# Softmax of the first q group moved partly onto ScalarE, searched ranks and later loads in an attention + feed-forward kernel

## Chip, cores and metric

One core of a Trainium2 chip. The metric is the device time of one execution in microseconds (us); a smaller time is better.

## What is computed

Linear attention with two softmaxes, then a feed-forward layer with a sigmoid-approximated gelu. q, k, v are float32 of shape 8 x 8 x 576 x 64 (batch, heads, rows, columns); the two weight matrices are float64.

```python
q_s = softmax of q over the last axis (64 columns), denominator + 1e-09
k_s = softmax of k over axis 2 (576 rows), denominator + 1e-09
kv  = einsum('bhsd,bhse->bhde', k_s, v)
x   = einsum('bhsd,bhde->bhse', q_s, kv), as 4608 rows x 512 columns
h   = x @ w_in                                # 512 x 2048
out = (h * (1 / (1 + exp(-1.702 * h)))) @ w_out   # 2048 x 512
```

## The kernel before

The 4608 rows are worked off in 12 blocks `t` of 384 rows (128 partitions x 3). Blocks 0 and 1 are special: their k, q and v are loaded in two groups of 4 heads each (`ek`, `eq`, `ev`, in memory that later holds weights), the later blocks in groups of 2 heads.

For a batch, `k_max` takes the maximum of k over rows (three VectorE steps and one reduction over partitions on GpSimd), `k_sub` subtracts it (L418, L421) and exponentiates on ScalarE (L424, L425), and `kv_pairs` multiplies k and v on TensorE (L465), with a column of ones for the sums, whose reciprocals (L470, L471) scale the result as ScalarE copies it out (L481). For a block, `q_soft` does the softmax of q for one group: maximum (L502) and subtraction (L503) on VectorE, one exponential over the whole group on ScalarE (L506), then sum, add, reciprocal and product on VectorE (L509 to L512). `q_tr` transposes (L529, copied out at L536), `x_pairs` multiplies by kv (L575 in the first two blocks), and `x_out` splits the result into a rounded part on ScalarE (L544) and a remainder on VectorE (L547).

The feed-forward layer takes 16 steps `j` per block: `g1` (L604, 12 matmuls of 384 columns; gelu at L610, rounding at L613, remainder at L616), and `g2` (L636, three pieces `c` of three matmuls of 512 columns). Both use split operands, so each product is three matmuls. Each of the 32 weight tiles (`wi0` to `wi15`, `wo0` to `wo15`, 512 KB each) arrives as float64 words and is converted once by `conv_w`: ScalarE L251, VectorE L255, L259 and L260, ScalarE L264, VectorE L270.

What sets the order: every step is entered in a list (`Plan.add`) with engine, cost, the buffers that it reads and writes, and a rank. `Plan.order` runs a small model of the engines (constants `HOP, LAND, RATE, ISSUE, TABLE`, L24) in which an engine that is free takes the ready step of lowest rank. The order in which steps begin in that model is the order in which the instructions are written, and each engine then works its own list strictly in that order. All loads are issued by SyncE (SP). Blocks 0 and 1 share steps 0 to 31 or so: `step_rank` lets their `g1` and `g2` alternate.

Of the kernel before, what the change touches and what calls it, by code (L numbers as in the profile page):

```python
# [18 lines left out]
class Plan:  # L19
# [1 line left out]

    HOP, LAND, RATE, ISSUE, TABLE = 0.1, 1.8, 270e3, 0.5, 1.28  # L24

    def __init__(self):
        self.ops = []
# [19 lines left out]
    def order(self):  # L47
        ops = self.ops
        left = [len(o[2]) for o in ops]
        users = [[] for _ in ops]  # L50
        for n, o in enumerate(ops):
            for d in o[2]:
                users[d].append(n)
        engines = sorted({o[0] for o in ops})
        free = dict.fromkeys(engines, 0.0)
        ready = {e: [] for e in engines}
        coming = []
        at = [0.0] * len(ops)
        for n, o in enumerate(ops):
            if not left[n]:  # L60
                heapq.heappush(ready[o[0]], (o[3], n))
        wire, table = 0.0, None
        began = []
        self.start = {}
        now = 0.0
        while len(began) < len(ops):
            while coming and coming[0][0] <= now:
                _, n = heapq.heappop(coming)
                heapq.heappush(ready[ops[n][0]], (ops[n][3], n))
            moved = False  # L70
            for e in engines:
                if free[e] > now or not ready[e]:
                    continue
                _, n = heapq.heappop(ready[e])
                _, cost, _, _, _, needs, size = ops[n]
                if needs is not None and needs != table:
                    cost, table = cost + self.TABLE, needs
                free[e] = done = now + cost
                if size:
                    wire = max(wire, done) + size / self.RATE  # L80
                    done = wire + self.LAND
                began.append(n)
                self.start[n] = now
                moved = True
                for u in users[n]:
                    left[u] -= 1
                    hop = 0.0 if ops[u][0] == e and not size else self.HOP
                    at[u] = max(at[u], done + hop)
                    if not left[u]:
                        heapq.heappush(coming, (at[u], u))  # L90
            if not moved:
                times = [f for e, f in free.items() if f > now and ready[e]]
                if coming:
                    times.append(coming[0][0])
                now = min(t for t in times if t > now) if any(t > now for t in times) else now
        return began


def dve(n, psum=False):
    return 0.15 + n / 960  # L100

# [6 lines left out]
def efficient_attention_then_gelu_ffn(  # L108
# [27 lines left out]
    ST = S - SM  # L136
    W = D + 1
    JOIN = 9

    const = ctx.enter_context(tc.tile_pool(name="const", bufs=1))  # L140
    psum = ctx.enter_context(tc.tile_pool(name="psum", bufs=1, space=bass.MemoryType.PSUM))
# [4 lines left out]
    def sb(name, shape, dtype=F32, tag=None):  # L146
        return const.tile(shape, dtype, name=name, tag=tag or name)
# [135 lines left out]
    def bc(a, n):  # L283
        return a.unsqueeze(len(a.shape)).broadcast_to([*a.shape, n])
# [4 lines left out]

    kbuf, vbuf, qbuf, tbuf = {}, {}, {}, {}  # L290

    def load_tail(b, rank):
        if b in etail:
            (kl, vl), tag = etail[b]
            keys = ((tag, 0), (tag, "v"))
        else:
            (kl, vl), keys = tail[0], ((("tail"), 0), (("tail"), 1))
        tbuf[b] = kl, vl, keys

        def run_k():  # L300
            nc.sync.dma_start(out=kl[0:ST], in_=k[b, :, SM:S, :].rearrange("h p d -> p h d"))  # L301

        def run_v():
            nc.sync.dma_start(out=vl[0:ST, :, 0:D], in_=v[b, :, SM:S, :].rearrange("h p d -> p h d"))  # L304

        plan.add("SP", plan.ISSUE, (), (keys[0],), rank, run_k, size=ST * H * D * 4)
        plan.add("SP", plan.ISSUE, (), (keys[1],), rank + 0.01, run_v, size=2 * ST * H * D * 4)

    def load_k(b, i, rank):
        n = group(b)  # L310
        t, key = ek[b, i] if b < 2 else (kt_[i], ("kt", i))
        kbuf[b, i] = t, key
        hs = slice(n * i, n * (i + 1))

        def run():
            nc.sync.dma_start(
                out=t.rearrange("p h c d -> p h (c d)"),
                in_=k[b, hs, 0:SM, :].rearrange("h (p c) d -> p h (c d)", c=CM),
            )

        plan.add("SP", plan.ISSUE, (), (key,), rank, run, size=n * SM * D * 4)

    def load_v(b, i, rank):
        n = group(b)
        t, key = ev[b, i] if b < 2 else (vt_[i], ("vt", i))
        vbuf[b, i] = t, key

        def run():
            if b < 2:
                nc.sync.dma_start(  # L330
                    out=t.rearrange("p h c d -> p h (c d)"),
                    in_=v[b, n * i : n * (i + 1), 0:SM, :].rearrange("h (p c) d -> p h (c d)", c=CM),
                )
                return
            for h in range(n):
                nc.sync.dma_start(
                    out=t[:, h, :, 0:D], in_=v[b, n * i + h, 0:SM, :].rearrange("(p c) d -> p c d", c=CM)
                )

        if b < 2:  # L340
            plan.add("SP", plan.ISSUE, (), (key,), rank, run, size=n * SM * D * 4)
        else:
            plan.add("SP", n * 0.6, (), (key,), rank, run, size=1.5 * n * SM * D * 4)

    def parts(t):

        t0 = t * TB
        b, s0 = divmod(t0, S)
        n = min(TB, S - s0)
        got = [(b, s0, 0, n // C)]  # L350
        if n < TB:
            got.append((b + 1, 0, n // C, P))
        return got
# [6 lines left out]
    def load_q(t, i, rank):  # L360
        n = group(t)
        qt, key = eq[t, i] if t < 2 else (qt_[i % 2], ("qt", i % 2))
        qbuf[t, i] = qt, key
        runs = [(0, 1, 1), (1, 0, 1)] if turned(parts(t)[0][0], i) else [(0, 0, n)]

        def run():
            for b, s0, p0, p1 in parts(t):
                for o, h, m in runs:
                    src = q[b, n * i + h : n * i + h + m, s0 : s0 + (p1 - p0) * C, :]
                    if t < 2:  # L370
                        nc.sync.dma_start(
                            out=qt[p0:p1].rearrange("p h c d -> p h (c d)"),
                            in_=src.rearrange("h (p c) d -> p h (c d)", c=C),
                        )
                    else:
                        nc.sync.dma_start(
                            out=qt[p0:p1, :, o : o + m], in_=src.rearrange("h (p c) d -> p c h d", c=C)
                        )

        plan.add("SP", plan.ISSUE * len(parts(t)) * len(runs), (), (key,), rank, run, size=n * TB * D * 4)  # L380

    nm = [0]
    maxes = {}
# [100 lines left out]

    nr = [0]
    rs = [sb(f"r{i}", [P, NP]) for i in range(2)]
    qm = [sb(f"qm{i}", [P, 4 * C]) for i in range(2)]

    def q_soft(t, i, ranks):
        n = group(t)  # L490
        qt, key = qbuf[t, i]
        M = ("qm", i % 2)
        dst, nkey = qt, key
        if t < 2:
            m = qm[i % 2].rearrange("p (h c) -> p h c", h=n)
            qn, nkey = qbuf[t, i] = en[t, i]
            dst = qn.rearrange("p c h d -> p h c d")
        else:
            m = qm[i % 2][:, : n * C].rearrange("p (c h) -> p c h", c=C)

        def run_m():
            nc.vector.tensor_reduce(out=m, in_=qt, axis=AX.X, op=ALU.max)  # L502
            nc.vector.tensor_tensor(out=qt, in0=qt, in1=bc(m, D), op=ALU.subtract)  # L503

        def run_e():
            nc.scalar.activation(qt, qt, AF.Exp)  # L506

        def run_s():
            nc.vector.tensor_reduce(out=m, in_=qt, axis=AX.X, op=ALU.add)  # L509
            nc.vector.tensor_scalar_add(m, m, 1e-9)  # L510
            nc.vector.reciprocal(m, m)
            nc.vector.tensor_tensor(out=dst, in0=qt, in1=bc(m, D), op=ALU.mult)  # L512

        e = n * C * D
        plan.add("DVE", 2 * dve(e), (key,), (key, M), ranks[0], run_m)
        plan.add("ACT", act(e), (key,), (key,), ranks[1], run_e, table="exp")
        plan.add("DVE", 2 * dve(e) + 0.35, (key,), (nkey, M), ranks[2], run_s)
# [234 lines left out]
    for rank, _, f, a in sorted(tasks, key=lambda s: s[:2]):  # L752
        if f in (load_k, load_v, load_q, k_max, k_sub, q_tr, x_pairs, g1, g2, load_w, conv_w, load_tail):
            f(*a, rank)
        else:
            f(rank)

    with tc.manual_schedule():
        for n in plan.order():
            plan.ops[n][4]()  # L760
# [24 lines left out]
```

## Time and profile before

| | |
|---|---|
| device time, median of 3 runs (range) | 916.12 us (915.61 to 918.11) |
| the profiled execution's own time | 916.58 us |
| its span, first to last instruction | 914.7 us |
| mean granted TensorE clock | 0.994 of full speed |
| TensorE busy | 885.1 us |
| VectorE, ScalarE busy | 390.2 us, 487.8 us |

The profiled execution is 0.46 us above the median; what lies around its span is 1.9 us. The profile page gives busy time per engine, a picture of the span in 40 slices, the chain of work that ended last, and the groups of instructions by source line. Times within the trace count from the start of the span.

### The profile page before, as it was taken

The page shows a single profiled execution, that of the slowest core. Times are in us where ns is not written, and L with a number is a line of the kernel's source. Part 1 is how long each engine was busy: PE and PEld are TensorE (multiplying, and loading weights), DVE is VectorE, ACT ScalarE, POOL GpSimd, SP SyncE. Part 2 cuts the span into 40 slices and gives each one's busy share as a digit, 9 for nine tenths or more (in the row PEclk, how much of TensorE's full clock was granted, in tenths as well). Part 3 has the DMA queues.
Part 4 walks back from the last instruction along what each step waited for, and adds up shares of the span by engine and source line. Part 5 has one row for each costly group of instructions (what it writes and reads, how often), then busy time and mean ns, then how long its engine had stood idle before and what let it go on. Part 6 is the DMA issues. An engine that isn't in the chain of part 4 may idle for free.

```text
span 914.7 us, 13010 instructions
## 1 busy us (share of the span) xinstructions
PE 885.1 (97%) x5200; PEld 785.7 (86%) x5200; DVE 390.2 (43%) x826; ACT 487.8 (53%) x840; POOL 27.8 (3%) x35
## 2 busy tenths in 40 slices
PE   2879999999999999999999999999999999999998
PEld 2668989888988988989889889888988898998897
DVE  8899996162531641341541352332263134132111
ACT  3776669464952763552773583544494265253222
POOL 1100001000100100000000010000010000000000
PEclk9899999999999999999999999999999999999999
DMA  9996000111310400000400320000141000000000
GB/s 257 353 315 208 1 1 1 52 53 31 100 40 14 120 11 35 18 18 35 122 18 34 85 55 35 18 18 35 33 100 42 9 18 9 36 18 1 35 1 35
DMA packets 94620, 55.37 MB, mean 61 GB/s; under 512 B 67424, under 2 KB 87904, under 8 KB 94560
## 3 DMA queue, kind: packets, MB, share of 16 engines
q1 hardware_dynamic: 94560, 54.54, 21.0%
q8 instruction: 41, 0.67, 0.3%
q14 instruction: 19, 0.16, 0.1%
HBM read 45.09 MB, written 9.44 MB: 60 GB/s over the span
## 4 chain that ended last, share of the span: by engine, by line
PE 93%; DMA 4%; SPq 2%; DVE 1%; ACT 0%; issue 0%; DVEq 0%
PE bank L636 44%; PE bank L604 44%; PE bank L465 2%; PE bank L529 1%; PE bank L580 1%; DMA raw<-in_moe_w_out 1%; DMA raw<-in_moe_w_in 1%; DMA ek<-in_k 1%; SPq L226 0%; PE bank L575 0%; SPq L221 0%; DVE tmp L260 0%; SPq L304 0%; DVE tmp L259 0%; SPq L330 0%; SPq L301 0%
## 5 line engine op out<-in xcount | busy, mean ns | idle before, releaser
L604 PE MATMUL bank<-xh,w 128*128 128x384 f32 x1536 | 429.0, 341 | 4.6 <-ACT w L264 3.5
L636 PE MATMUL bank<-w,gh 128*128 128x512 f32 x1152 | 366.6, 399 | 0.0
L604 PEld LDWEIGHTS bank<-xh,w 128*128 128x128 f32 x1536 | 282.0, 189 | 14.7 <-ACT w L264 3.9
L616 DVE TENSOR_TENSOR gl<-g,gh 128x384 fp32r<-128x384 f32 x192 | 106.6, 556 | 385.0 <-ACT gh L613 384.3
L610 ACT ACTIVATE g<-bank 128x384 f32<-128x384 f32 x192 | 94.5, 492 | 326.8 <-PE bank L604 326.0
L604 PE MATMUL bank<-xl,w 128*128 128x384 f32 x768 | 259.7, 338 | 0.0
L636 PEld LDWEIGHTS bank<-w,gh 128*128 128x128 f32 x1152 | 214.5, 189 | 41.1 <-issue 4.4
L636 PE MATMUL bank<-w,gl 128*128 128x512 f32 x576 | 228.4, 397 | 0.0
L604 PEld LDWEIGHTS bank<-xl,w 128*128 128x128 f32 x768 | 144.9, 189 | 7.0
L636 PEld LDWEIGHTS bank<-w,gl 128*128 128x128 f32 x576 | 108.7, 189 | 25.8
L613 ACT CAST gh<-g 128x384 fp32r<-128x384 f32 x192 | 98.5, 513 | 6.3 <-PE bank L636 0.3
L610 ACT ACT_TABLE_LOAD x54 | 69.3, 1283 | 1.0
L502 DVE TENSOR_REDUCE qm<-qt 128x6 f32<-128x384 f32 x40 | 22.0, 551 | 67.2 <-DMA qt<-in_q 67.2
L506 ACT ACT_TABLE_LOAD x36 | 46.2, 1283 | 1.9 <-DMA qt<-in_q 1.3
L403 POOL PARTITION_ALL_REDUCE mx<-mx x24 | 21.0, 876 | 611.1 <-DVE mx L399 611.1
L536 ACT COPY qT<-bank 128x384 f32<-128x384 f32 x48 | 22.7, 476 | 29.8 <-PE bank L529 29.6
L509 DVE TENSOR_REDUCE qm<-qt 128x6 f32<-128x384 f32 x40 | 22.0, 550 | 25.7 <-ACT qt L506 25.6
L424 ACT ACT_TABLE_LOAD x18 | 23.1, 1283 | 5.5 <-DMA ek<-in_k 5.2
L465 PE MATMUL bank<-ev,ek 128*64 128x64 f32 x128 | 7.2, 273 | 19.0 <-ACT eq L506 12.4
L547 DVE TENSOR_TENSOR xl<-bank,xh 128x384 fp32r<-128x384 f32 x48 | 24.0, 550 | 3.0 <-ACT xh L544 3.0
L481 ACT ACTIVATE kvn<-bank,r 64x64 f32<-64x64 f32 x64 | 17.9, 306 | 14.0 <-DVE r L471 12.2
L251 ACT ACTIVATE tmp<-raw 128x512 f32<-128x512 f32 x32 | 21.2, 673 | 5.7 <-DVE w L270 5.6
(71 smaller groups left out, 495.4 us busy)
## 6 DMA issues: line engine op xcount, KB each, us to landing
out<-tmp SPq DMA_DIRECT2D x36, 256.0 KB, 2.1
raw<-in_moe_w_in SPq DMA_DIRECT2D x16, 512.0 KB, 10.0
raw<-in_moe_w_out SPq DMA_DIRECT2D x16, 512.0 KB, 10.2
kt<-in_k SPq DMA_DIRECT2D x24, 256.0 KB, 4.1
vt<-in_v SPq DMA_DIRECT2D x48, 128.0 KB, 4.0
qt<-in_q SPq DMA_DIRECT2D x36, 96.0 KB, 2.7
qt<-in_q SPq DMA_DIRECT2D x16, 192.0 KB, 2.9
ek<-in_k SPq DMA_DIRECT2D x4, 512.0 KB, 7.5
```

What stands on the lines that cost most here:

```text
L424: nc.scalar.activation(t, t, AF.Exp)
L465: nc.tensor.matmul(pk[r0 : r0 + D, m, cols], lhs, rhs, start=c == 0, stop=c == CM, tile_position=(0, r0))
L502: nc.vector.tensor_reduce(out=m, in_=qt, axis=AX.X, op=ALU.max)
L506: nc.scalar.activation(qt, qt, AF.Exp)
L509: nc.vector.tensor_reduce(out=m, in_=qt, axis=AX.X, op=ALU.add)
L536: nc.scalar.copy(qT, pq[:, :TB])
L547: nc.vector.tensor_tensor(out=xl, in0=px[:, :TB], in1=xh.bitcast(F32), op=ALU.subtract)
L604: nc.tensor.matmul(ph, wi[w][j][:, c, :], x[:, c, :], start=c == 0 and i == 0, stop=c == KC - 1 and i == 2,)
L610: nc.scalar.activation(gt, ph, AF.Gelu_apprx_sigmoid)
L613: nc.scalar.copy(gh, gt)
L616: nc.vector.tensor_tensor(out=gl, in0=gt, in1=gh.bitcast(F32), op=ALU.subtract)
L636: nc.tensor.matmul(po[c], x[:, cs], wo[w][j], start=j == 0 and i == 0, stop=j == NJ - 1 and i == 2)
```

## The change

Four things change.

1. **q softmax of group 0 in blocks 0 and 1** (`QACT`). VectorE takes the negated maximum only. ScalarE then does 12 exponentials of 128 x 64, one for each head and row of a partition, each with that row's negated maximum as bias, and each gives the row's sum as well. VectorE adds 1e-9, takes the reciprocal and multiplies. The VectorE subtraction over 768 columns and the VectorE sum over 768 columns are gone for these two groups. Group 1 of both blocks is as before.
2. **Ranks.** The steps whose rank is below 12 (268 in number: all of the first two blocks' attention, the weights and the first steps of the feed-forward layer) get ranks from a table of numbers, `FIRST`, in place of those of the loops.
3. **Loads of the third block.** The loads of batch 2 on and of q from block 2 on are entered as reading all tiles that hold block 1's early buffers, that is, they come after all weight loads.
4. **Constants of the planner's model** (landing 1.8 to 2.2, rate 270e3 to 330e3, issue 0.5 to 0.6, SP free from 0.7).

```diff
-    HOP, LAND, RATE, ISSUE, TABLE = 0.1, 1.8, 270e3, 0.5, 1.28
+    HOP, LAND, RATE, ISSUE, TABLE = 0.1, 2.2, 330e3, 0.6, 1.28
...
-        free = dict.fromkeys(engines, 0.0)
+        free = dict.fromkeys(engines, 0.0) | {"SP": 0.7}
...
+FIRST = [
+    557, -9000, -8950, -8949, -8900, -8800, -8700, -8600, -8500, -8400, -8350, -8300, -8250, -8249, -8200, -8100,
...
+]
...
+    QACT = {(0, 0), (1, 0)}
...
+    def behind(late):
+
+        return tuple((tag, 0) for tag, b in held.items() if b == 1) if late else ()
...
-        plan.add("SP", plan.ISSUE, (), (key,), rank, run, size=n * SM * D * 4)
+        plan.add("SP", plan.ISSUE, behind(b > 1), (key,), rank, run, size=n * SM * D * 4)
...
+    sums = [sb(f"qs{i}", [P, 4 * C]) for i in range(2)]
...
+        if (t, i) in QACT:
+
+            flat = qt.rearrange("p h c d -> p (h c d)")
+            mf, sf = qm[i % 2], sums[i % 2]
+
+            def run_n():
+                nc.vector.tensor_reduce(out=m, in_=qt, axis=AX.X, op=ALU.max, negate=True)
+
+            def run_a():
+                for x in range(n * C):
+                    w = flat[:, x * D : (x + 1) * D]
+                    nc.scalar.activation(w, w, AF.Exp, bias=mf[:, x : x + 1], accum_out=sf[:, x : x + 1])
+
+            def run_z():
+                nc.vector.tensor_scalar_add(sf, sf, 1e-9)
+                nc.vector.reciprocal(sf, sf)
+                nc.vector.tensor_tensor(
+                    out=dst, in0=qt, in1=bc(sf.rearrange("p (h c) -> p h c", h=n), D), op=ALU.mult
+                )
+
+            Q = ("qs", i % 2)
+            plan.add("DVE", dve(e), (key,), (M,), ranks[0], run_n)
+            plan.add("ACT", 0.30 * n * C, (key, M), (key, Q), ranks[1], run_a, table="exp")
+            plan.add("DVE", dve(e) + 0.4, (key, Q), (nkey, Q), ranks[2], run_z)
+            return
...
+    begun = [n for n, o in enumerate(plan.ops) if o[3] < 12]
+    assert len(begun) == len(FIRST)
+    for n, r in zip(begun, FIRST):
+        e, cost, deps, _, run, table, size = plan.ops[n]
+        plan.ops[n] = e, cost, deps, r / 100, run, table, size
```

Where the order moves, at three places. Each line gives source line (after the change all lines are further down), operation, and written tile <- read tiles. `ek_121`, `ek_129` are block 0's k, groups 0 and 1, `ek_126`, `ek_134` block 1's; `eq_122`, `eq_130` and `eq_127`, `eq_135` the q of block 0 and of block 1; `ev_125`, `ev_133` block 0's v.

**SyncE, the first loads.** Before:

```order
L316 DMA ek_121<-in_k 128x4x256
L301 DMA et<-in_k 64x8x64
L304 DMA et<-in_v 64x8x64
L316 DMA ek_129<-in_k 128x4x256
L371 DMA eq_122<-in_q 128x4x192
L371 DMA eq_130<-in_q 128x4x192
L330 DMA ev_125<-in_v 128x4x256
L330 DMA ev_133<-in_v 128x4x256
L221 DMA raw<-in_moe_w_in 128x4x256
L226 DMA raw<-in_moe_w_out 128x1024
```

Now:

```order
L345 DMA ek_121<-in_k 128x4x256
L330 DMA et<-in_k 64x8x64
L333 DMA et<-in_v 64x8x64
L246 DMA raw<-in_moe_w_in 128x4x256
L345 DMA ek_129<-in_k 128x4x256
L400 DMA eq_122<-in_q 128x4x192
L400 DMA eq_130<-in_q 128x4x192
L359 DMA ev_125<-in_v 128x4x256
L359 DMA ev_133<-in_v 128x4x256
L246 DMA raw<-in_moe_w_in 128x4x256
L251 DMA raw<-in_moe_w_out 128x1024
```

A weight load (it is `wi1`) stands ahead of the second group of k, so every load from there to the last of block 0's v comes one load of 512 KB later; the two weight loads `wi0`, `wo0` follow v as before.

**ScalarE, from block 0's last copies to the first gelus.** Before, beginning with the conversion of the third weight:

```order
L251 ACTIVATE tmp_85<-raw 128x512
L424 ACTIVATE ek_126<-ek_126 128x1024
L425 ACTIVATE kl_105<-kl_105 64x256
L610 ACT_TABLE_LOAD
L610 ACTIVATE g_77<-bank_68 128x384
L613 CAST gh_81<-g_77 128x384
L264 CAST w<-tmp_85 128x512
L251 ACTIVATE tmp_86<-raw 128x512
L506 ACT_TABLE_LOAD
L506 ACTIVATE eq_127<-eq_127 128x768
L251 ACTIVATE tmp_87<-raw 128x512
L251 ACTIVATE tmp_85<-raw 128x512
```

Now, beginning at the same kind of step:

```order
L276 ACTIVATE tmp_86<-raw 128x512
L536 ACTIVATE eq_135<-eq_135 128x768
L276 ACTIVATE tmp_85<-raw 128x512
L556 ACTIVATE eq_127,qs_144<-eq_127,qm_146 128x64 x12
L453 ACTIVATE ek_126<-ek_126 128x1024
L454 ACTIVATE kl_105<-kl_105 64x256
L665 ACT_TABLE_LOAD
L665 ACTIVATE g_78<-bank_67 128x384
L668 CAST gh_83<-g_78 128x384
L665 ACTIVATE g_77<-bank_68 128x384
L668 CAST gh_81<-g_77 128x384
```

Two conversions (of `wo1` and `wo2`) and all exponentials of block 1's q, the 12 small ones among them, now stand ahead of the exponential of block 1's first k, and two gelus follow on one table load, where a table load stood on either side of the exponential of `eq_127`.

**VectorE, around the remainders `xl_73` of block 0.** Before:

```order
L547 TENSOR_TENSOR xl_73<-bank_65,xh_72 128x384
L547 TENSOR_TENSOR xl_73<-bank_66,xh_72 128x384
L397 TENSOR_TENSOR em<-ek_126 128x512
L398 TENSOR_TENSOR em<-em 128x256
L399 TENSOR_TENSOR em<-em,kl_105 64x256
L547 TENSOR_TENSOR xl_73<-bank_65,xh_72 128x384
L270 TENSOR_TENSOR w<-tmp_87,w 128x512
L547 TENSOR_TENSOR xl_73<-bank_66,xh_72 128x384
L418 TENSOR_TENSOR ek_126<-ek_126,em 128x1024
```

Now:

```order
L602 TENSOR_TENSOR xl_73<-bank_66,xh_72 128x384
L295 TENSOR_TENSOR w<-tmp_87,w 128x512
L532 TENSOR_REDUCE qm_147<-eq_135 128x12
L533 TENSOR_TENSOR eq_135<-eq_135,qm_147 128x768
L602 TENSOR_TENSOR xl_73<-bank_66,xh_72 128x384
L426 TENSOR_TENSOR em<-ek_126 128x512
L427 TENSOR_TENSOR em<-em 128x256
L428 TENSOR_TENSOR em<-em,kl_105 64x256
L295 TENSOR_TENSOR w<-tmp_85,w 128x512
L602 TENSOR_TENSOR xl_73<-bank_65,xh_72 128x384
```

The maximum and subtraction of `eq_135` and the third converted weight (`tmp_85`, L295) now stand ahead of the last two remainders.

## Rows read from the trace of the kernel before

**Rows 1.** Profile page, part 1: busy us (share of span), instructions.
```profile
PE 885.1 (97%) x5200; PEld 785.7 (86%) x5200; DVE 390.2 (43%) x826; ACT 487.8 (53%) x840; POOL 27.8 (3%) x35
```

**Rows 2.** Busy time by stretch, TensorE: window, length, busy (count), PEclk, DMA share, GB/s.
```profile
66.00:910.00 844.00, 843.93 (x4774) 1.00 0.15 41
```

**Rows 3.** Waits of TensorE over the span: total us, times, longest.
```profile
PE bank L465 <- ACT eq L506: 12.4, 1, 12.4
PE bank L465 <- ACT ek L424: 6.6, 3, 3.7
PE bank L604 <- ACT w L264: 3.5, 2, 2.4
```

**Rows 4.** The chain that ended last, 66 to 78 us: start, us, what.
```profile
66.07 2.64 PE bank L604 x10
68.71 3.03 PE bank L636 x9
71.74 4.24 PE bank L604 x24
75.98 2.11 PE bank L636 x9
```

**Rows 5.** DMA issues of v's groups, issued 4.86 and 5.87: KB, us to landing.
```profile
ev<-in_v SPq DMA_DIRECT2D x1, 512.0 KB, 7.4
...
ev<-in_v SPq DMA_DIRECT2D x1, 512.0 KB, 7.9
```

**Rows 6.** TensorE in order of time: start, us, operation, [idle before <- releaser].
```profile
12.44 1.12 PE L465 MATMUL bank<-ev,ek 128*64 128x64 f32 x16 [12.44 <-ACT eq L506]
...
14.56 1.13 PE L465 MATMUL bank<-ev,ek 128*64 128x64 f32 x16
...
36.06 0.69 PE L465 MATMUL bank<-ev,ek 128*64 128x64 f32 x16 [1.41 <-ACT ek L424]
...
37.25 0.66 PE L465 MATMUL bank<-ev,ek 128*64 128x64 f32 x16
...
39.68 0.51 PE L604 MATMUL bank<-xh,w 128*128 128x384 f32 x1 [1.11 <-ACT w L264]
...
44.51 1.05 PE L636 MATMUL bank<-w,gh 128*128 128x512 f32 x2
...
47.62 0.49 PE L529 MATMUL bank<-ident,en 128*128 128x128 f32 x3
```

**Rows 7.** Groups of VectorE instructions, first 80 us: busy us, mean ns | idle before.
```profile
L270 DVE TENSOR_TENSOR w<-tmp,w 128x512 fp32r<-128x512 f32 x12 | 8.2, 684 | 0.1
...
L547 DVE TENSOR_TENSOR xl<-bank,xh 128x384 fp32r<-128x384 f32 x8 | 4.3, 553 | 1.6 <-ACT xh L544 1.6
L503 DVE TENSOR_TENSOR eq<-eq,qm 128x768 f32<-128x768 f32 x4 | 3.8, 958 | 0.1
...
L509 DVE TENSOR_REDUCE qm<-eq 128x12 f32<-128x768 f32 x4 | 3.8, 946 | 0.9 <-ACT eq L506 0.9
...
L397 DVE TENSOR_TENSOR em<-ek 128x512 f32<-128x512 f32 x4 | 2.7, 686 | 0.4 <-DMA ek<-in_k 0.4
L398 DVE TENSOR_TENSOR em<-em 128x256 f32<-128x256 f32 x4 | 1.7, 425 | 0.1
```

**Rows 8.** TensorE in a window of the first slow stretch, columns as in rows 2.
```profile
42.00:44.00 2.00, 2.00 (x8) 0.50 1.08 358
```

**Rows 9.** Groups of ScalarE instructions, first 80 us: busy us, mean ns | idle before.
```profile
L481 ACT ACTIVATE kvn<-bank,r 64x64 f32<-64x64 f32 x16 | 5.0, 310 | 1.5 <-DVE r L470 1.3
...
L506 ACT ACTIVATE eq<-eq 128x768 f32<-128x768 f32 x4 | 3.4, 840 | 3.6 <-DVE eq L503 3.6
```

**Rows 10.** Products of q and kv in block 1, first 80 us: busy us, mean ns.
```profile
L575 PE MATMUL bank<-qT,kvn 128*128 128x192 f32 x16 | 3.3, 339 | 0.0
```

**Rows 11.** VectorE's first work on block 2, in order of time.
```profile
134.44 0.55 DVE L502 TENSOR_REDUCE qm<-qt 128x6 f32<-128x384 f32 x1
```

**Rows 12.** DMA issue of weight `wo1`, issued at 22.70: KB, us to landing.
```profile
raw<-in_moe_w_out SPq DMA_DIRECT2D x1, 512.0 KB, 10.4
```

More of the change, by code (lines that the diff above doesn't have):

```diff
@@ L304, in run_v @@
             nc.sync.dma_start(out=vl[0:ST, :, 0:D], in_=v[b, :, SM:S, :].rearrange("h p d -> p h d"))
-        plan.add("SP", plan.ISSUE, (), (keys[0],), rank, run_k, size=ST * H * D * 4)
-        plan.add("SP", plan.ISSUE, (), (keys[1],), rank + 0.01, run_v, size=2 * ST * H * D * 4)
+        plan.add("SP", plan.ISSUE, behind(b > 1), (keys[0],), rank, run_k, size=ST * H * D * 4)
+        plan.add("SP", plan.ISSUE, behind(b > 1), (keys[1],), rank + 0.01, run_v, size=2 * ST * H * D * 4)
     def load_k(b, i, rank):
@@ L342, in load_v @@
         else:
-            plan.add("SP", n * 0.6, (), (key,), rank, run, size=1.5 * n * SM * D * 4)
+            plan.add("SP", n * 0.6, behind(True), (key,), rank, run, size=1.5 * n * SM * D * 4)
     def parts(t):
@@ L378, in run @@
                         )
-        plan.add("SP", plan.ISSUE * len(parts(t)) * len(runs), (), (key,), rank, run, size=n * TB * D * 4)
+        plan.add("SP", plan.ISSUE * len(parts(t)) * len(runs), behind(t > 1), (key,), rank, run, size=n * TB * D * 4)
     nm = [0]
```

16 rows, old and new, of the table FIRST are left out of this document.

## Prediction

> **What bounds the kernel now.** I read the page's busy times first: TensorE is busy 97% of the span, VectorE 43%, ScalarE 53% [rows 1]. Then the busy time by stretch: from 66 us to 910 us TensorE is busy 843.93 of 844.00 us at full clock [rows 2]. So nothing can be won behind 66 us unless TensorE's work gets less, and the change leaves every matmul as it is. The third view, TensorE's waits, says where the rest lies: 12.4 us before the first matmul, and some 13 us in small waits, mostly for k's exponential (6.6) and for converted weights (3.5) [rows 3]. All of them end by 66.1 [rows 4]. The first wait is put down to ScalarE's exponential of q, but the first matmul doesn't read q: it reads v, issued at 4.86 and landed 7.4 later, at 12.26, and it starts at 12.44 [rows 5, 6].
>
> What stands behind the small waits is VectorE. In the first 80 us the idle times beside its groups are small [rows 7], and it has both the softmaxes and the conversion of the weights to do. There the change takes work away.
>
> A second loss is the clock. After the waits of 1.41 and 1.11 us the granted clock is 0.50, which is 1.2 of 2.4 GHz [rows 6, 8]. The price is in the rows: the twelve matmuls of a `g1` take 4.24/2 = 2.1 us at full clock and 44.51 - 39.68 = 4.8 in the slow stretch, of which 0.6 is a wait, so 2.1 too much; the nine of a `g2` take 2.11 at full clock, 47.62 - 44.51 = 3.1 there, 1.0 too much [rows 4, 6]. A second, shorter stretch at 66.07 costs another 0.9 on a `g2` (3.03 against 2.11) and about 0.7 on the `g1` ahead of it [rows 4]. Together 3.1 + 1.6 = 4.7 us.
>
> **The change, part by part.** *VectorE's relief.* Each of the two groups loses a subtraction (0.96 us) and a sum (0.95) [rows 7]: 2 x 1.9 = 3.8 us, in a stretch where VectorE has no slack. *ScalarE's burden.* One exponential of 0.84 us becomes twelve of 64 columns. The trace has no such instruction. The nearest row is the scaled copy at L481, also 64 columns with a value per partition: 0.31 us, and I take 0.32 with the step to the next one, 3.8 us a group [rows 9]. Bounds: at least the 0.84 of the one instruction; at most two such instructions each, if the sum is a step of its own, 12 x 0.64 = 7.7. In return the new order has two loads of ScalarE's table less before 65 us; some dozen more later on lie under TensorE's work.
>
> *The early weight.* One 512 KB load goes ahead of v. The two groups of v, issued one behind the other, landed at 12.26 and 13.77 [rows 5], so such a load is worth 1.5 us of queue, and the first matmul comes at 13.9: 1.5 later.
>
> *The new order.* I walked the new order by hand: each instruction starts when its engine is free and the last of its inputs is there, with the durations of the groups in the trace.
> - 13.9: the first two k-v products, 14.56 - 12.44 = 2.1 each [rows 6], end at 18.1. The third needs the bank that the second one's scaled copy empties; ScalarE has its twelve exponentials and k's behind it until 17.7, and the copy ends at 19.2.
> - Transposes and products of block 0 then end near 30.9 (32.1 before).
> - The first `g1` needs the last remainder. On VectorE there stand ahead of the last two remainders, from about 30.1: maximum and subtraction of `eq_135` (1.9), a remainder (0.5), the maximum of k (0.69 + 0.43 + 0.4 = 1.5), a weight's last step (0.6) and the last remainder (0.5) [rows 7]. That gives 35.2: a wait of 4.3 us for TensorE, new, where 32.1 was enough before. But two `g1` follow back to back, to 39.4, since the early weight is converted by then.
> - ScalarE meanwhile does its twelve exponentials from 36.1 to 40.0 and k's to 41.3. So block 1's k-v products start at 41.35 (36.06 before [rows 6]); TensorE waits 2.0.
> - Then 1.6 for the first remainder of the gelu; `g2` starts at 45.7. From there I find no wait over 0.2 us. Work in the list up to the first `g1` of block 1: twelve pieces of `g2` at 0.7 (8.4), two `g1` (4.2) [rows 4], two k-v products at 37.25 - 36.06 = 1.2 (2.4) [rows 6], four q-kv products, 3.3 [rows 10], and three sets of transposes, an estimate of 1.2: between a quarter of a `g2` piece and a whole one each. With 0.4 of waits that is 19.9, hence 65.6.
>
> **The sum.** Before, the same `g1` starts at 71.7, with nine `g2` pieces done [rows 4]. Now it starts at 65.6 with twelve done, 2.1 us more work. At full clock TensorE is 71.7 - 65.6 + 2.1 = 8.2 us ahead, and behind that point both orders keep it busy, so the lead reaches the end unchanged. From it comes the clock: the 4.3 us of waiting, and waits of 2.0 and 1.6 behind it, are longer than those ahead of the slow stretch before. I take one such stretch, at its price of 3.1 us, on the two `g1` and what follows. 8.2 - 3.1 = 5.1 us. The profiled execution took 916.58, which gives 911.5; it stands 0.46 above the median of the runs, so against the median of 916.12 I say **911.0**.
>
> Parts that I cost at nothing: the third block's loads go behind the weights. In the trace VectorE takes up that block's q first at 134.4 us [rows 11], and all loads that now go ahead of it were issued by 75, so tens of us cover it; without that cover each us of lateness would cost one. The planner's constants act through the order alone.
>
> **The rivals.**
> *A, the clock holds.* If the two `g1` run at full clock the lead stays near 8.2: 908.0. For it: in the trace the clock fell after a stretch of short matmuls with waits between, not after a single wait. Chance 0.13.
> *B, the clock stays low longer.* A slow stretch from the first `g1` until about 52 us, or both stretches as before: 4.7 to 5.0 off the lead, 912.8. For it: five waits remain between 17 and 46 us. Chance 0.20. In "TensorE: Matmul & The Clock Gate" (Part 1) the Trainium skill says that throttled is the default state and that activity releases it. By that rule the wait of 4.3 us alone puts both `g1` at 1.2 GHz, 2 x 2.1 = 4.2 us off the lead and a time of 912.1; the rows before show a fall after two shorter waits and agree.
> *C, the small exponentials are dear.* At 0.64 each (the bound above) ScalarE is 3.9 us later in each block. By the walk the lead at full clock shrinks to 1.8, and the slow stretch then lies inside the waits: 914.3. Chance 0.10.
> *D, weights hold up ScalarE: slower.* ScalarE works in order, and ahead of `eq_135`'s exponential, the twelve small ones and k's there now stands the first conversion of `wo1`, then that of `wo2`. `wo1` landed at 22.70 + 10.4 = 33.1 before [rows 12], and the same bytes stand ahead of it now; I need it at 33.1 and `wo2` 1.5 later. Each us that these land later puts the exponentials, block 1's products and all behind them later by one. From 5.1 us on the kernel is slower; at 8 us late, 919.0. Against it: the loads are the same in number and size. For it: that slack is thin, and the walk has no other work for ScalarE there. Chance 0.08.
> *E, the waits only change places.* The walk hides hops between engines; if every one of some fifteen handovers on the way costs 0.3 more than I took, the lead is gone: 916. Chance 0.07.
>
> **How the numbers follow.** The forecast case has 0.42, by itself 909.5 to 912.3. A measurement of this kernel can tell about 0.3%, 2.7 us, from no change, so faster means below 913.4 and slower above 918.9. Faster: forecast, A and nearly all of B, 0.74. Within 0.3%: C, E and small parts of B and D, 0.18. Slower: most of D and what I have not seen, 0.08. The range runs from 907.5 (A with a little more) to 915.5 (past C); outside are D, E and the far end of A, under 0.2.
>
> **What would show it.** In the changed kernel's profile: the first matmul near 13.9; twelve exponentials of 128 x 64 at about 0.32 apart; a wait of some 4 us before the first `g1`, near 35; granted clock 0.5 somewhere between 35 and 45 and 1.0 after; no wait of TensorE over 0.5 us after 51; the first `g1` of block 1 between 65 and 69, with twelve `g2` pieces ahead of it; four table loads before 66 us, not six. The prediction is wrong if TensorE still waits between 52 and 66 us, if the exponentials are over 0.45 each, or if ScalarE's idle time before a conversion of `wo1` or `wo2` ends on a DMA later than 35 us.

## The result and the profile after

The changed kernel takes 907.39 us (median of 4 runs, 905.33 to 908.44) against 915.87 (915.45 to 918.11): a ratio of 0.9896 with a 95% interval from 0.9881 to 0.991 (the two medians alone give 0.9907, inside it). It is 8.5 us faster; I had forecast 5.1. The profiled executions stand at 916.58 and 907.42, their spans at 914.7 and 905.3 us, 9.4 apart. The next lines say where the 9.4 lie.

TensorE's waits in the changed kernel (us in total, times, longest), which answer to [rows 3]:

```profile
PE bank L494 <- DMA ev<-in_v: 13.9, 1, 13.9
PE bank L659 <- DVE xl L602: 1.8, 1, 1.8
PE bank L494 <- ACT kvn L510: 1.2, 1, 1.2
PE bank L494 <- ACT ek L453: 1.1, 1, 1.1
PE bank L630 <- ACT qT L591: 0.7, 1, 0.7
PE bank L691 <- ACT gh L668: 0.6, 1, 0.6
PE bank L691 <- DVE gl L671: 0.4, 1, 0.4
```

The first wait is 1.5 us longer, as an early weight goes ahead of v. Of the some 13 us of waits behind it, about 6 are left. The chain of work that ended last, where block 1 begins in the changed kernel (start, us, what), answers to [rows 4]:

```profile
65.66 2.80 PE bank L691 x12
68.45 6.26 PE bank L659 x36
```

The first `g1` of block 1 starts at 68.45, where it was 71.74, and by then twelve pieces of `g2` are done where nine were. Three pieces are 2.1 us. The lead at this place is 71.74 - 68.45 + 2.1 = 5.4 us, and the forecast's sum was 5.1. Behind it TensorE has no idle time, as before [rows 2] (window, length, busy with counts of PE, PEld, DVE, ACT and POOL, PEclk, DMA share, GB/s):

```profile
68.00:900.00 832.00, 832.00 (x4746) 743.26 (x4746) 327.01 (x702) 459.39 (x773) 18.97 (x24) 1.00 0.14 38
```

So 9.4 - 5.4 = 4.0 us came in a part where both kernels keep TensorE busy without a gap, at full clock, with the same matmuls. They must take less time each. The chain at the same place of a later block, in the kernel before:

```profile
490.50 2.09 PE bank L636 x9
492.59 2.12 PE bank L604 x12
494.71 2.11 PE bank L636 x9
496.82 2.12 PE bank L604 x12
498.94 2.11 PE bank L636 x9
501.05 2.08 PE bank L604 x12
```

and in the changed kernel:

```profile
483.17 2.08 PE bank L691 x9
485.25 2.09 PE bank L659 x12
487.34 2.08 PE bank L691 x9
489.42 2.09 PE bank L659 x12
491.51 2.10 PE bank L691 x9
493.61 2.08 PE bank L659 x12
```

Here a `g1` (x12) or `g2` (x9) takes 0.01 to 0.03 us less, until the last row, which is 2.08 in both. The groups of matmuls between 100 and 880 us say the same in means that are easy to overlook; before:

```profile
L604 PE MATMUL bank<-xh,w 128*128 128x384 f32 x1397 | 388.2, 339 | 0.0
L636 PE MATMUL bank<-w,gh 128*128 128x512 f32 x1048 | 332.1, 398 | 0.0
```

and changed:

```profile
L659 PE MATMUL bank<-xh,w 128*128 128x384 f32 x1400 | 387.3, 338 | 0.0
L691 PE MATMUL bank<-w,gh 128*128 128x512 f32 x1055 | 333.0, 396 | 0.0
```

Matmuls overlap, so these means show the direction and not the amount. Counted from the start of one group to the start of the next (groups between 100 and 880 us that stand alone), a `g1` takes 2107.9 ns in the mean for 2120.4, a `g2` 2099.3 for 2109.4. That is 22.6 ns a pair, and some 188 of the 192 pairs lie behind 68 us: 4.2 us, about what is sought.

It is not spread evenly. The times depend on `j` and repeat from block to block (86% of the groups lie within 2 ns of the median for their `j`): before, `g1` takes 2115 to 2118 ns for `j` 0 to 4 and 11, and 2082 to 2084 for 5, 6, 9 and 10. The slow ones use the weight tiles that get their memory last: `wi0` to `wi4`, `wi11`, `wi12` and `wo0` to `wo6`. The other 18 take over memory of the first blocks' k, q and v. The two new sum tiles (48 bytes a partition, laid in 64 each) stand ahead of those last 14 and move them up by 128 bytes. In the compiled programs they begin 32 bytes behind a multiple of 256 before, 160 after; the other 18 begin at 64 and the tiles of x and g at 128 in both.

### The profile page after: what moved, and what is told of

Read it like the earlier page. It is cut to its first block, busy times and chain, and to the rows that moved or that the text cites. A ratio compares the mean times of both kernels' runs of the same rounds, so it can differ in the third digit from the quotient of the medians.

```text
span 905.3 us, 13074 instructions
## 1 busy us (share of the span) xinstructions
PE 881.2 (97%) x5200; PEld 784.7 (87%) x5200; DVE 385.3 (43%) x822; ACT 508.3 (56%) x896; POOL 24.8 (3%) x35
## 4 chain that ended last, share of the span: by engine, by line
PE 96%; DVE 2%; DMA 1%; SPq 1%; ACT 0%; issue 0%; DVEq 0%
PE bank L691 45%; PE bank L659 44%; PE bank L494 3%; PE bank L584 2%; PE bank L635 1%; PE bank L630 1%; DMA ev<-in_v 1%; DVE en L561 0%; SPq L400 0%; DVE tmp L284 0%; DVE tmp L285 0%; DVE em L426 0%; DVE ek L447 0%; DVE xl L602 0%; ACT xh L599 0%
## 5 line engine op out<-in xcount | busy, mean ns | idle before, releaser
L591 ACT COPY qT<-bank 128x384 f32<-128x384 f32 x48 | 22.6, 478 | 32.7 <-PE bank L584 32.6
L432 POOL PARTITION_ALL_REDUCE mx<-mx x24 | 19.0, 791 | 600.9 <-DVE mx L428 600.9
L599 ACT CAST xh<-bank 128x384 fp32r<-128x384 f32 x48 | 20.1, 486 | 10.3 <-PE bank L630 8.1
L289 ACT CAST w<-tmp 128x512 fp32r<-128x512 f32 x32 | 19.6, 620 | 9.8 <-DVE tmp L285 9.2
```

The lines of the kernel that those rows point to most:

```text
L591: nc.scalar.copy(qT, pq[:, :TB])
```

## The experiments

**1. Place or order?** Theory 1: the 4.0 us come from where those 14 tiles lie. Theory 2: from the new order of instructions. Four runs, with one edit each to the line of `sums`:

```diff
 e1 (on the kernel before)
+    sums = [sb(f"qs{i}", [P, 4 * C]) for i in range(2)]
 e2 (on the changed kernel)
-    sums = [sb(f"qs{i}", [P, 4 * C]) for i in range(2)]
+    sums = [m1_[:, 4 * C * i : 4 * C * (i + 1)] for i in range(2)]
 e3 (as e2) and e4 (on the kernel before), behind qm
+    sb("pad", [P, 1])
```

> The kernel before, with nothing new but the two small tiles of sums, which no instruction touches. They lie ahead of the 14 weight tiles that are placed last and shift these by 128 bytes, to the place that they have in the changed kernel. Theory 1 (the 3.9 us that the dense part gained come from where those tiles lie): the dense part takes the pace of the changed kernel, a g1 of j 0 to 4 falls from 2115-2118 ns to 2089-2097, a g2 of j 0 to 6 from 2103-2111 to 2082-2095, the first g1 of block 1 stays at 71.7 us, and the time is 916 - 3.9 = 912 us. Theory 2 (they come from the new order of instructions): the pieces keep their 2115 and 2109 ns, and the time stays at 916.

> The changed kernel, with the sums put into a tile that lies idle then, so that the 14 weight tiles lie as in the kernel before. Theory 1 (place of the tiles): first g1 of block 1 still at 68.3 us, but a g1 of j 0 to 4 takes 2115-2118 ns again and a g2 of j 0 to 6 2103-2111, and the time is 907.4 + 3.9 = 911.3 us. Theory 2 (order of the instructions): the pieces stay at 2089-2097 and 2082-2095 ns and the time at 907.4.

> As the last one, with 32 bytes left empty ahead of the 14 weight tiles, which then begin at a multiple of 64 bytes like the other 18. Theory 1, in the form that a multiple of 64 is what counts: all g1 without transposes ahead of them take 2080-2085 ns, j 0 to 4 and 11 too, some 0.08 us a block less than in the changed kernel, and the time is 906.4 us. If only the distance from the place before counts and 32 bytes are too little, the pieces are as in the kernel before and the time 911. Theory 2: 907.4.

> The kernel before with the same 32 bytes left empty, and no sums. Theory 1 with multiples of 64: the dense part as in the run before this one, first g1 of block 1 at 71.7 us, time 916 - 3.9 - 1.0 = 911 us. Theory 2: 916.

Measured, against 916.65 us for the kernel before (9 runs): e1 912.9 us (ratio 0.996, 0.9947 to 0.9972), e2 910.43 (0.9936, 0.9923 to 0.9948), e3 907.33 (0.9895, 0.988 to 0.991), e4 912.24 (0.9955, 0.9942 to 0.9967). Two tiles that nothing touches make the kernel before 3.8 us faster. Without their shift the changed kernel gains 6.2 us for 8.5. The chain of e2 has the old pace back:

```profile
487.29 2.12 PE bank L659 x12
489.41 2.11 PE bank L691 x9
491.51 2.12 PE bank L659 x12
493.63 2.11 PE bank L691 x9
495.74 2.08 PE bank L659 x12
```

Theory 2 falls for the greater part. Behind the first `g1` of block 1, at full clock, e2 takes 840.1 us (68.81 to 908.9) and the changed kernel, with the same order, 836.9 (68.45 to 905.3). That is 3.2 us by the places alone; e1 against the kernel before gives 3.3 (839.7 for 843.0). The remaining 0.7 of the 4.0 us lies between the two orders, and no run shows what makes it.

With a multiple of 64, e4 and e3 end where e1 and the changed kernel do: `g1` gets faster than there (2083 ns for nearly all `j` without transposes ahead), `g2` slower (2094 to 2097). The 1.0 us that I had expected on top did not come, so "multiples of 64" is not the rule.

**2. Which part of the change makes the other 5 to 6 us?** These runs hold the order of every engine fixed (the list that the planner made is written into the kernel) and keep the tiles where the changed kernel has them.

```diff
 e5 (order of the changed kernel)
-    QACT = {(0, 0), (1, 0)}
+    QACT = set()
 e6 (order of the kernel before, with q_soft's new branch)
+    QACT = {(0, 0), (1, 0)}
 e7 (order of the changed kernel): load_q(2, 0), load_q(2, 1), load_k(2, *) and
    load_v(2, *) moved from behind all weight loads to behind that of wi9
```

> The changed kernel's order of work, held fixed on every engine, and its places of tiles, but the first group of q in blocks 0 and 1 as before: subtract and sum on VectorE, one long exponential on ScalarE. VectorE gets 2 x (0.96 + 0.95) = 3.8 us more by the rows of before, ScalarE some 6 us less. Theory (VectorE's relief is where the front's 5 us come from): most of the 3.8 us return, 909.5 to 911.2 us. Rival (the new order alone does it): 907.4 within 1 us.

> The reverse: the order of the kernel before, held fixed, with the tiles placed as in the changed kernel (the run with the tiles shifted took 912.9 us), and only the exponentials of the first group head by head. Theory (VectorE's relief): up to 3.8 us less than 912.9, so 909.1 to 911 us. Rival (in the old order the 24 short exponentials hold ScalarE up, and the relief is lost): 912.9 or above.

> The changed kernel's order, held fixed, but the ten loads of the third block's q, k and v go back among the weight loads, behind that of wi9, about where the kernel before has them. They are some 3 MB, about 9 us at 330 GB/s, ahead of seven weight loads. Theory (these loads were worth nothing, the prediction gives them no term): 907.4 within 0.7 us. Rival (weights that land later stop the conversions on ScalarE and VectorE): 1 to 4 us more, 908.5 to 911.5.

e5 took 910.99 us (0.9941, 0.9928 to 0.9953), e6 913.3 (0.997, 0.9959 to 0.9981), e7 907.12 (0.9899, 0.9883 to 0.9915), the kernel before 916.48. Measured from e1, which has the same places (912.9): the new order alone gives 1.9 us, the short exponentials alone nothing, both together 5.5. Taking the short exponentials out costs 3.6, near VectorE's 3.8. By the intervals of the ratios each of these differences is uncertain by 1.5 to 1.8 us, so they don't show that a us of VectorE's time is worth a us of the kernel's. TensorE's waits in e5 show where a part of the 3.6 goes:

```profile
PE bank L584 <- DVE en L542: 3.8, 2, 2.5
PE bank L659 <- DVE xl L602: 2.6, 1, 2.6
PE bank L691 <- DVE gl L671: 1.9, 1, 1.9
```

All three end on VectorE: on the product that ends q's softmax (0.3 us in the changed kernel) and on two remainders. The clock has a part too: in e5 the second slow stretch fills the windows from 48 to 54 us (0.57, 0.50, 0.50), in the changed kernel those from 48 to 52 (0.65, 0.50).

In e6 the relief is there: between 30 and 66 us VectorE is busy 28.65 us, in e1 33.22. It is worth nothing that can be measured: TensorE's waits add up to 26.2 us, in e1 to 26.0. Two windows (columns as above; DVE is the third busy time, ACT the fourth):

```profile
42.00:44.00 2.00, 2.00 (x11) 1.73 (x11) 0.09 (x1) 2.00 (x13) 0.00 (x0) 1.00 1.09 351
44.00:46.00 2.00, 0.77 (x4) 0.29 (x2) 1.29 (x3) 2.00 (x7) 0.00 (x0) 1.00 1.10 348
```

and the wait of VectorE that lies in them (start, us, instruction, idle before):

```profile
44.65 0.17 DVE L531 TENSOR_SCALAR qs<-qs 128x12 f32<-128x12 f32 x1 [2.56 <-ACT eq L528]
```

In the old order the second twelve exponentials meet a ScalarE that has no pause, and VectorE stands idle for 2.56 us for want of its results. That this is what uses the relief up is argued from one trace, and e6's is that of the slowest of its seven executions (915.88 us). The late loads of the third block are worth nothing that can be measured, as the prediction had it.

**3. What about the place sets the pace?** e8 spreads the 14 tiles over eight offsets; e9 puts all 14 at 128 behind a multiple of 256, e10 all 32; e11 shifts the whole memory by 96 bytes from the first tile on.

```diff
 e8, in place of the line of qm (r and qm go into the idle tile `first`)
+    for y in ("wi0", "wi1", "wi2", "wi3", "wi4", "wi11", "wi12", "wo0", "wo1", "wo2", "wo3", "wo4", "wo5", "wo6"):
+        sb(f"at{y}", [P, 2 * DM], I32, tag=y)
+        if y not in ("wo5", "wo6"):
+            sb(f"pad{y}", [P, 1])
 e9 (as e2), behind qm
+    sb("pad", [P, 24])
 e10 (as e3), ahead of the first early tile
+    sb("padall", [P, 16])
 e11 (as e2), ahead of ident
+    sb("padall", [P, 24])
```

> The changed kernel's order, with the 14 weight tiles that were placed last now at offsets from a multiple of 256 bytes that differ by 32: those of w_in with j 0, 1, 2, 3, 4, 11, 12 at 96, 128, 160, 192, 224, 0, 32, and those of w_out with j 0 to 6 at 64, 96, 128, 160, 192, 224, 224. If the place of the tile a g1 or g2 reads sets its pace: g1 of j 1, 3, 11 (multiples of 64) at 2083 ns, j 2 (160) at 2089-2097, j 12 (32) 2115 and 90 more for the transposes ahead of it, j 0 and 4 (96, 224) in between; g2 of j 0 (64) at 2097, j 3 (160) at 2082-2095. If only the distance between tiles or the load order counts, no such pattern by offset.

> The changed kernel with the sums in an idle tile and 96 bytes left empty, so that all 14 weight tiles that are placed last begin 128 bytes behind a multiple of 256, where the run of eight places had its fastest pieces (g1 2082 ns, g2 2076). If the place alone sets the pace: g1 of j 0 to 4 and 11 at 2082-2083 for 2089-2097 in the changed kernel, g2 of j 0 to 6 at 2076-2084 for 2082-2095; 0.09 + 0.04 to 0.09 us a block, 1.6 to 2.1 us in twelve blocks, 905.3 to 905.8. If the pieces at their sides set it as much, no better than the aligned run, 907.3.

> The same with all 32 weight tiles at 128 bytes behind a multiple of 256, the 18 others too, which have been at 64. If the place alone sets the pace: g1 stays at 2082-2085, g2 of j 7 to 15 falls from 2090-2097 to 2076-2084, another 0.07 to 0.14 us a block, 903.6 to 905. If 64 and 128 are alike for these: as the last run.

> The changed kernel with the tiles laid as in the run with the sums in an idle tile (weights at 32 and 64 behind a multiple of 256, x and g at 128), and the whole lot moved up by 96 bytes: weights at 128 and 160, x and g at 224. If the distance between a weight tile and x or g sets the pace, the pieces are as in that run, g1 of j 0 to 4 at 2115-2117 and of j 5, 6, 9 at 2083-2085. If the address of the weight tile alone does, they change places: j 0 to 4 (128) about 2082, j 5, 6, 9 (160) about 2090 to 2098.

e8 took 907.58 us in one execution. Its `g1` with `j` 0 to 4 (offsets 96, 128, 160, 192, 224) took 2083, 2082, 2098, 2117 and 2093 ns, `j` 11 (offset 0) 2107. So offset counts, but for `g1` 192, a multiple of 64, is the slowest, while the `g2` whose tile lies at 192 (`j` 4) is one of the two fastest, at 2075 (2076 at 128). e9 took 905.63 (0.9882, 0.9865 to 0.9899), e10 906.82 (0.9894, 0.9877 to 0.991), the kernel before 916.46; e11 took 909.91 in one execution. Its chain is that of e2:

```profile
486.10 2.12 PE bank L660 x12
488.22 2.11 PE bank L692 x9
490.33 2.12 PE bank L660 x12
492.44 2.11 PE bank L692 x9
```

All 32 of its `g1` and `g2` times agree with e2's within 2 ns, though no tile of weights, x or g has kept its address or its offset. So, over this shift of 96 bytes, the address of a tile by itself counts for nothing; what counts is how the tiles lie to each other. The medians over the blocks, in ns, with offsets behind a multiple of 256:

| run | last 14 tiles | other 18 | x and g | `g1`, j 0-4 | `g1`, j 5, 6, 9 | `g2`, j 0-6 |
|---|---|---|---|---|---|---|
| before, e2 | 32 | 64 | 128 | 2115-2118 | 2082-2084 | 2102-2111 |
| e11 | 128 | 160 | 224 | 2115-2118 | 2082-2084 | 2102-2111 |
| changed, e1 | 160 | 64 | 128 | 2089-2097 | 2085 | 2082-2095 |
| e3, e4 | 64 | 64 | 128 | 2083-2084 | 2083 | 2094-2097 |
| e9 | 128 | 64 | 128 | 2082-2106 | 2084 | 2076-2081 |
| e10 | 128 | 128 | 128 | 2102-2106 | 2106 | 2080-2088 |
| e12 | 64 (`w_in`), 128 (`w_out`) | the same | 128 | 2084 | 2084 | 2076-2081 |

e3 and e10 differ only in the distance between the weights and x and g: with 64 bytes of it (modulo 256) `g1` is fast and `g2` slow, with none the reverse. e9 shows that the pieces at the sides count too: its `w_in` tiles for `j` 0 to 4 all lie at 128, and `g1` takes 2106 ns where the `w_out` tiles of the neighbouring `g2` lie at 128 as well (`j` 3, 4), 2082 to 2092 (`j` 0 to 2) where at least one of them is at 64. The 10 ns between `j` 0 and `j` 1, both with neighbours at 64, stay unexplained. And the whole times of e3, e9 and e10 can't be set against each other for the places, since they reach block 1's first `g1` at 69.67, 67.18 and 66.40 us.

**4. The best places of those tried.** The last run takes the fast half of e3 and of e10:

```diff
 e12 (as e2): at_tags lays a tile for each name; ahead of the early tiles, then behind qm
+    at_tags(f"wi{j}" for j in (5, 6, 7, 8, 9, 13, 14, 15, 10))
+    sb("padmid", [P, 1])
+    at_tags(f"wo{j}" for j in range(7, 16))
...
+    at_tags(f"wi{j}" for j in (0, 1, 2, 3, 4, 11, 12))
+    sb("padlast", [P, 16])
+    at_tags(f"wo{j}" for j in range(7))
```

> The changed kernel's order, the sums in an idle tile, all 16 tiles of w_in at 64 and all 16 of w_out at 128 bytes behind a multiple of 256, with x and g at 128 as ever. If the distance between a weight tile and the x or g it meets sets the pace: g1 as in the aligned run (2083 ns without transposes ahead, mean 2103.5), g2 as in the run with all tiles at 128 (2080 to 2088, mean 2088.7), so 15 ns less than in the changed kernel for each of 192 pairs, 2.9 us: 904.5, and below the 905.6 of the fastest version so far. If which tiles lie side by side counts beyond that, g1 or g2 come out slower and the time is 905.6 to 907.5.

It took 902.05 us (901.64 to 904.27; the kernel before 915.61; ratio 0.9853, 0.983 to 0.9876): 13.6 us faster than the kernel before, 5.3 faster than the change. Its chain:

```profile
479.33 2.08 PE bank L701 x9
481.41 2.08 PE bank L669 x12
483.49 2.08 PE bank L701 x9
485.57 2.08 PE bank L669 x12
```

The mean `g1` takes 2104.1 ns, the mean `g2` 2084.5, so 18.6 ns a pair less than in the changed kernel, 3.6 us over 192 pairs. That is more than I had expected (2.9). The rest of the 5.3 lies ahead of 68 us, where its profiled execution reaches block 1's first `g1` at 66.51 and not at 68.45. The order there is the same; what differs in the two traces is the clock. In e12 it falls once, between 36 and 40 us, and the second slow stretch of the changed kernel, at 48 to 52, is missing:

```profile
48.00:50.00 2.00, 1.69 (x11) 1.19 (x10) 2.00 (x4) 1.75 (x5) 0.00 (x0) 1.00 1.07 385
```

The clock varies so between executions of one order (below), so this rest is not shown to be a gain of the places.

## Why the prediction was right up to block 1 and too small behind it

- **The bound, and what VectorE's relief is worth: right in size.** The two groups' 3.8 us came back as 3.6 in e5, with some 1.7 of uncertainty and a part of the clock in it. What I didn't see is that the relief needs the new order: by itself it is worth nothing that can be measured (e6).
- **The early weight: right.** The first matmul was to start at 13.9 and starts at 13.89.
- **The twelve exponentials: right, with a step that I had only as a bound.** I took 0.32 us from one to the next and it is 0.33. The sum does come as an instruction of its own (groups of ScalarE, first 80 us):

```profile
L556 ACT ACTIVATE eq<-eq,qm 128x64 f32<-128x64 f32 x24 | 8.0, 336 | 2.4 <-DVE qm L551 2.4
...
L556 ACT ACTIVATION_READ_ACCUMULATOR eq<-eq,qm 128x1 f32 x24 | 4.5, 189 | 0.0
```

  But it runs beside the next exponential, so rival C's 0.64 for each doesn't arise.
- **The wait ahead of the first `g1`: right in kind, wrong in place.** I had the whole `g1` wait to 35.2. It reads x piece by piece: it starts at 32.77 and waits 1.83 us in its middle for the last remainder, which comes at 37.24. This is two us later than walked; on the way to it, block 0's products end at 33.6 and not at 30.9.
- **The clock: near in size, by other stretches.** I took one slow stretch at 3.1 us on the two `g1` and what follows. PEclk shows two, the second from 48 to 52, where I had expected 1.0 (columns as above):

```profile
38.00:40.00 2.00, 2.00 (x9) 2.00 (x8) 2.00 (x4) 1.87 (x11) 0.00 (x0) 0.59 1.05 375
40.00:42.00 2.00, 2.00 (x7) 1.71 (x6) 1.90 (x5) 2.00 (x13) 0.00 (x0) 0.56 1.09 376
46.00:48.00 2.00, 0.98 (x5) 0.35 (x3) 1.93 (x6) 1.94 (x6) 1.06 (x1) 1.00 1.12 352
48.00:50.00 2.00, 2.00 (x7) 1.65 (x8) 1.86 (x4) 1.73 (x5) 0.00 (x0) 0.65 1.05 385
50.00:52.00 2.00, 2.00 (x8) 1.81 (x7) 2.00 (x4) 1.46 (x4) 0.00 (x0) 0.50 1.03 384
```

  TensorE is busy all through these four slow windows, and what they lose is 2 x (0.41 + 0.44 + 0.35 + 0.50) = 3.4 us. With it the lead at full clock is 5.4 + 3.4 = 8.8; the walk had 8.2.

  A third slow part is missing from the column and from my working. The packed trace has no clock record ahead of 34.94 us in the changed kernel and of 29.67 in the kernel before, and where it has none a window is printed as 1.00. The matmuls show the level themselves. Two of 384 columns in the changed kernel, ahead of 34.94 and in a slow window:

```profile
33.99 0.84 PE L659 MATMUL bank<-xh,w 128*128 128x384 f32 x2
38.82 0.84 PE L659 MATMUL bank<-xh,w 128*128 128x384 f32 x2
```

  and in the kernel before, at full clock:

```profile
32.73 0.52 PE L604 MATMUL bank<-xh,w 128*128 128x384 f32 x2
```

  So from the first matmul on both kernels ran at the lower level, the changed one 5.3 us longer, and the mean clock of 0.994 in the table of before leaves this out. [rows 6] had the sign of it: the k-v product that takes 2.1 us at 12.44 takes 1.2 at 36.06, and I used both numbers without asking why. The four products at the end of block 0, on the way to the last remainder, take 2.93 us from 30.62; two of them took 0.91 in the kernel before, at 30.47. By that I estimate that 1.1 us of the lateness at 33.6 is the clock's.
- **The lead at block 1: near, in part by luck.** 5.1 in the sum, 5.4 in the trace, with products that end later than walked, a shorter wait and other slow stretches. In the nine profiled executions that issue block 0's and block 1's work in the changed kernel's order (the changed kernel, e2, e3, e7 to e12), block 1's first `g1` starts between 66.40 (e10) and 69.67 (e3), which makes the lead 7.4 to 4.2. It goes with the first clock record: in the six that reach full clock at 29.1 to 30.7 us this `g1` starts by 67.81, in the three that reach it at 34.6 to 35.9 it starts at 68.45 or later. Why the clock rises early or late is not shown. e2, which has the old places, gains 6.2 (4.8 to 7.1 by its interval).
- **The step that failed: "behind that point both orders keep it busy, so the lead reaches the end unchanged".** Both do keep it busy, but they don't take the same time for the same work. I read "the change leaves every matmul as it is" from the source and took it that its duration stays too. The change adds two tiles of 48 bytes a partition, these move 14 weight tiles by 128 bytes, and each pair of `g1` and `g2` gets 22.6 ns shorter: 4.0 us, of which e1 and e2 put 3.2 to 3.3 on the places. It is a term that the sum lacked and no rival had, and the chances of the forecast and the five rivals add up to 1.00, so nothing was left for it. The rows were there to make one suspicious: in the trace of before the same `g1` takes 2.12 us with one `j` and 2.08 with another.
- **Rivals.** A gave nearly the right time, 908.0, for the wrong reason: the clock did fall. B is what the clock did in form, two stretches with the last to 52 us; its price was 4.7 to 5.0, and those two cost 3.4. In "TensorE: Matmul & The Clock Gate" (Part 1) the Trainium skill says that throttled is the default state and that activity releases it. The rows agree in kind: the lower level stands at the start, and both later stretches follow waits, of 1.83 us and of 1.14 and 0.61. They don't agree with the 4.2 us that I worked out by it for two `g1`: the first of the two stretches cost 2 x (0.41 + 0.44) = 1.7. D and E did not happen: no conversion of `wo1` or `wo2` waits for a load, and no wait of TensorE over 0.5 us is left behind 47.

## What to carry to other kernels

Where an engine is busy without a gap, don't take its pace as given: look in the chain whether equal groups of work take equal times, and if the difference goes with the tile that they read, try where the tiles lie. A change that allocates anything, or that alters the order in which tiles first get their memory, moves tiles as well; to learn what its own steps are worth, run it once with the tiles where they were, and run the old kernel once with the new places. And relief for a busy engine that puts work on another one paid here only in an order that had room for it there. Read the clock from the durations of equal matmuls as well: a window printed as 1.00 can be one without a record.

## What the runs showed of the hardware that I had not expected

- Matmuls of 128 x 128 by 384 or 512 columns in split float32, each with a new weight load, run at a pace that depends on how the tiles in SBUF lie to each other: 2082 to 2118 ns for the same twelve and 2075 to 2111 for the same nine, mostly steady to 2 ns over the blocks, and unchanged if everything moves together by 96 bytes (e11). The Trainium skill says in "TensorE: Matmul & The Clock Gate" (Part 2, step 1) that loading the next tile's weights takes no read bandwidth from the running matmul, as TensorE has two read ports of its own. These runs don't show which accesses meet. But e3 beside e10, where only the distance between the two operands' tiles differs, shows that where the operands lie changes the pace. If it is those two reads that meet, the page's sentence doesn't hold here, and the measurement decides. That 256 is the period was not shown by itself; it is the number by which the runs can be put in one table.
- An exponential with a sum beside it is two instructions on ScalarE, 0.34 and 0.19 us, that start 0.33 us apart from one pair to the next.
- TensorE's first rise to full clock comes at 29.1 us (e12) to 35.9 us (e3) in profiled executions with the same order ahead of it, and block 1's first `g1` at 66.40 to 69.67 (e10, e3), so differences of an us in this part need several runs.
